# Attention with normed q and k, then a squared-ReLU product: another order of work in the first twelve pairs of heads

## The chip, the cores and the metric

The kernel runs on one core of a Trainium2 chip. The metric is the time of one execution on the device in microseconds (us); of several executions the median is taken. All times below are in us unless marked ns.

## The reference

q, k and v have 8 batches, 12 heads, 448 rows and 64 columns. q and k are normed row by row, attention is a plain softmax, and the heads side by side are the input of a two-layer product.

```python
def rmsnorm(x, g):
    return x / np.sqrt(np.mean(x * x, axis=-1, keepdims=True) + 1e-06) * g
q_n, k_n = rmsnorm(q, g_q), rmsnorm(k, g_k)
scores = np.matmul(q_n, k_n.transpose(0, 1, 3, 2)) / np.sqrt(64)
attn = softmax(scores)                       # exp, divided by its sum
x = heads_side_by_side(attn @ v)             # (8*448, 768)
h = np.maximum(x @ w_in, 0.0)                # w_in (768, 2048)
out = (h * h) @ w_out                        # w_out (2048, 768)
```

q, k and v come as 4-byte floats. w_in and w_out come as 8-byte floats, so the kernel takes each number apart into two 4-byte words and makes a 4-byte float of it on the chip.

## The kernel before, in words

**Tiling.** Two heads are a pair: 48 pairs in all, 6 per batch. Two batches make a span, so there are 4 spans of 12 pairs. Keys are cut into four chunks of 112. `scores(i, c)` (L748) computes for chunk c of pair i the two heads' scores into one of two banks of PSUM and turns them into exponentials with ScalarE. In the first 12 pairs the scale of k sits in that exponential (L759), so k is transposed raw and only q is normed beforehand. `values(i, chunks)` (L805) multiplies exponentials with v into `pav`; `add_up(i, c)` (L766, one VectorE add at L769) sums exponentials over chunks; `total_of(i)` (L813) sums the result over keys with a matmul against ones (L819); `finish(i)` (L822) inverts the sum and scales `pav` into `xT` (L832 to L839); `combine_x(i)` (L842) makes differences of `xT` that the product needs. The `pav` of even pairs lies in a bank of its own, that of odd pairs in bank "n", one of two banks ("m", "n") that the transposes of pairs and, later, the product use as well (`bank`, L456).

**The two products** of a span work with seven products of half-size blocks in place of eight (A11, S2, S1, S3, A12, A22, S4), on a 2 by 2 partition of weights and inputs. `first_product` (L956) has 8 rounds (f) of 7 steps, 56 steps of six matmul records each (L989). `second_product` (L1012) follows. Their weight blocks are streamed from DRAM into five buffers `sw` by `load_blocks` (L637, transfer at L651).

**Weights.** Before they can be streamed they must be made once. `prepare(t)` (L548) is one tick: it takes weight piece t (128 rows, 768 numbers of 8 bytes) through its steps. A tick is cut into four quarters, and `weights(upto)` (L622) runs quarters until that many have been issued. Quarter 1 has the write of a finished pair of pieces to DRAM (L588) and one VectorE step (L593); quarter 2 a ScalarE step (L596) and a VectorE step (L598); quarter 3 a VectorE step (L603) and GpSimd work on the pieces before (L574, L568); quarter 4 a ScalarE step for the next piece (L580), GpSimd work (L568, L574) and the loads of further pieces. The last tick, number 34, ends at quarter 140 (`ALL`). Pieces wait in words buffers: one place in `gC`, two in `gT` and the others in a pool.

**The order of the work** is written out by hand: every engine runs its own instructions in the order in which the program issues them, and waits on semaphores for the others. `attention_alone` (L856) issues the first 12 pairs (NAT = 12) and yields four times per pair. The caller (L1093) runs quarters of weights at each yield, up to `EARLY`. After that `first_product` for span 0 runs the rest of the quarters, spread over its steps (L1105). In all later spans attention is mixed with the second product by another function (L898).

In `attention_alone`, before the change, the first weights are loaded by SP's queue ahead of pair 2, and one tick of weights is issued (`weights(4)`, L1092) ahead of the first scores. Inside pair i come: the loads of pair i+3, scores 0 and 1, `norm(i+2)`, the add of chunk 1, a yield; then the k transpose of pair i+1, the rest of the values and the sum of pair i-1, the q transpose of pair i+1 (L742), `finish(i-1)`, the load of v, a yield; then scores 2 and 3, the first half of the values, a yield; then the add of chunk 2, `combine_x(i-1)`, a yield.

`norm(i)` (L689) squares q and k on ScalarE (L698), sums them on VectorE (L699, L700), takes the power -1/2 on GpSimd (L702) and multiplies q on GpSimd (L704). For pair 1 `normalise_in_turn` (L328) does q first and then k, each with half the work (L332 to L335), and multiplies q on VectorE (L338). From pair 12 on `norm` takes another way (L713: L718 to L726). SP's transfers for pair i+3 (L315, L325) write over what pair i+1 has used, so they wait for its norm.

Of the kernel before, what the change touches and what calls it, by code (L numbers as in the profile page):

```python
# [9 lines left out]
F32 = mybir.dt.float32  # L10
# [376 lines left out]
def attention_then_ffn_bounded(  # L387
# [37 lines left out]
    B, H, S, D = q.shape  # L425
    NT, DM = out.shape
    DFF = w_in.shape[1]
    P = 128
    NJ = 4
# [50 lines left out]
    stage = gC.rearrange("p i f n -> p (i f n)")  # L480
    NW = NPAIR * P
    HW = HC * P
    WORDS, BLOCKS, EXPS, LAST = 6, 2, 4, 31

    EARLY, ALL = 4 * 13, 4 * (2 * NFC + 3)
    assert DM == NW and BLOCKS * 8 * HW + EXPS * NW + 2 * NW <= 3 * HF * S and 2 * NW <= 4 * S and HF % 4 == 0


# [7 lines left out]
        both = words.rearrange("p (n two) -> p n two", two=2)  # L496
        return both[:, :, 0], both[:, :, 1]

    def place_of(n):

        return n % WORDS if n < LAST else 3

    def words_of(n):
        place = place_of(n)
        if place == 0:
            at = BLOCKS * 8 * HW + EXPS * NW
            flat = stage[:, at:at + 2 * NW]
        elif place < 3:
            f = (NFC, HF)[place - 1] - 2
            flat = gT[:, f:f + 2, :].rearrange("p f n -> p (f n)")[:, 0:2 * NW]  # L510
        else:
# [28 lines left out]

    def load_words(t, done):

        while loaded[0] <= t + 3 and all(
                place_of(m) != place_of(loaded[0]) for m in range(max(done, 0), loaded[0])):
            load_w(loaded[0])
            loaded[0] += 1

# [141 lines left out]
    def norm(i):  # L689
        if i >= NAT:  # L690
            squares(i)
            return norm_by_squares(i)
        raw, sq = (places_of(qk, i, n)[:SP] for n in range(2))
        rstd = rstds[i] = small.tile([SP, 2, 2 * NJ], F32, tag="rstd", name="rstd", bufs=4)
        normed[i] = sq[:, 0], raw[:, 1]
        if i == 1:
            return normalise_in_turn(nc, raw, sq, rstd, mhalf)
        nc.scalar.activation(sq, raw, AF.Square)  # L698
        nc.vector.tensor_reduce(rstd, sq.rearrange("p s (n d) -> p s n d", d=D), AX, ALU.add)  # L699
        nc.vector.tensor_scalar(rstd, rstd, 1.0 / D, 1e-6, ALU.mult, ALU.add)  # L700
        flat = rstd.rearrange("p s n -> p (s n)")
        nc.gpsimd.tensor_tensor(flat, flat, mhalf[:SP, 0:4 * NJ], ALU.pow)  # L702

        nc.gpsimd.tensor_tensor(sq[:, 0].rearrange("p (j h d) -> p h j d", j=NJ, h=2),  # L704
                                raw[:, 0].rearrange("p (h j d) -> p h j d", j=NJ, h=2),
                                rstd[:, 0].rearrange("p (h j) -> p h j ()", h=2).to_broadcast([SP, 2, NJ, D]),
                                ALU.mult)
# [55 lines left out]
    def acc_of(i):  # L763
        return sums[i % 2] if i < NAT else sums["acc"]
# [48 lines left out]
    def total_of(i):  # L813


        tots[i] = ps_o.tile([P, S], F32, tag="t", name="tot")
        for n, pr in enumerate((acc_of(i)[:SP], probs[i, NJ - 1])):
            for h in range(2):
                nc.tensor.matmul(tots[i][h * D:(h + 1) * D, :], sums["ones"], pr[:, h, :],  # L819
                                 start=(n == 0), stop=(n == 1))  # L820

    def finish(i):  # L822

        b, hp = divmod(i, NPAIR)
        pav, factors = pavs.pop(i), xT[:, b % 2, hp]
        x = factors
        if i < NAT:


            turned, factors = sums["turned"], sums["factors"]  # L830
            few = small.tile([P, S // 32], F32, tag="few", name="few")
            nc.vector.transpose(turned, tots.pop(i))  # L832
            nc.vector.reciprocal(few, turned.rearrange("p (g r) -> p g r", r=32)[:, :, 0])
            nc.vector.transpose(factors.rearrange("p (g r) -> p g r", r=32),
                                few.rearrange("p g -> p g ()").to_broadcast([P, S // 32, 32]))

            x = x.rearrange("d (p j) -> d j p", j=NJ)
            pav, factors = (t.rearrange("d (j p) -> d j p", j=NJ) for t in (pav, factors))
        nc.vector.tensor_tensor(x, pav, factors, ALU.mult)  # L839
        del vs[i]  # L840
# [15 lines left out]
    def attention_alone():  # L856


        for i in range(NAT):
            more = i + 1 < NAT  # L860
            if i + 3 < NAT:
                load(i + 3)
            scores(i, 0)
            scores(i, 1)
            if i + 2 < NAT:
                norm(i + 2)
            elif not more:
                norm(NAT)
                load(NAT + 2)
            add_up(i, 1)  # L870
            yield
            if i:
                transpose(i + 1, 1, 0) if more else None
                values(i - 1, (2, 3))
                total_of(i - 1)
                transpose(i + 1, 0, 0) if more else None
                finish(i - 1)
            load_v(i + 1)
            yield
            scores(i, 2)  # L880
            scores(i, 3)
            if i == 0:
                transpose(1, 0, 0)
                transpose(1, 1, 1)
            values(i, (0, 1))
            yield
            add_up(i, 2)
            if i:
                combine_x(i - 1)
            if NAT <= i + 3 < NAT + 2:  # L890
                load(i + 3)
            yield
        values(i, (2, 3))
        total_of(i)
        finish(i)
        combine_x(i)

# [58 lines left out]
    def first_product(work, span):  # L956
# [11 lines left out]
        for f in range(HF):  # L968
            n = span * (N1 + N2) + f * 7
            g11, g12 = gT[:, f, 0:S], gT[:, f, S:2 * S]  # L970
            g21, g22 = gT[:, HF + f, 0:S], gT[:, HF + f, S:2 * S]
            add = nc.vector.tensor_tensor
            ps_of = {}
            for i in range(7):

                into, rhs = {A11: ("pa", B11), S2: ("pb", T2), S1: ("pc", T1), S3: ("pd", T3),
                             A12: ("pa", B21), A22: ("pd", T4), S4: ("pc", B22)}[i]
                first = into not in ps_of
                if first and into == "pa":
                    if span == 0 and f:  # L980
                        ps_of[into] = ps_o.tile([P, S], F32, tag="ot"[f % 2], name="pa")
                    else:
                        ps_of[into] = ps_s.tile([P, 2, 512], F32, tag="s", name="pa")[:, 0, 0:S]
                elif first:
                    ps_of[into] = bank(into)
                ps = ps_of[into]
                load_blocks(n + i + 5)
                for c in range(HC):
                    nc.tensor.matmul(ps, stream[n + i][:, c], rhs[:, c], start=first and c == 0,  # L989
                                     stop=c == HC - 1, skip_group_check=not first)  # L990
                if i == A11:
                    p1 = work.tile([P, S], F32, tag="p1", name="p1")
                    nc.scalar.copy(p1, ps)
                elif i == S2:
                    z = work.tile([P, S], F32, tag="z", name="z")
                    add(z, p1, ps, ALU.add)
                elif i == S1:
                    y = work.tile([P, S], F32, tag="y", name="y")
                    add(y, z, ps, ALU.add)
                elif i == A12:  # L1000
                    activate(g11, ps)
                else:
                    g, x = {S3: (g22, y), A22: (g21, z), S4: (g12, z)}[i]
                    add(g, x, ps, ALU.add)  # L1004
                    activate(g, g)
                if span and f and i in (S1, A22):
                    combine(f - 1, (int(i == A22),))
                if span and f == HF - 1 and i == S4:
                    combine(f)
                yield  # L1010
# [65 lines left out]
            squares(nxt + 2)  # L1076

    with tc.tile_pool(name="words", bufs=2) as spare["pool"]:
        for _ in range(2):
            load_w(loaded[0])  # L1080
            loaded[0] += 1
        load(2)
        norm(1)
        with tc.tile_pool(name="first", bufs=2, reuse_waits="tile") as work:

# [3 lines left out]
            sums["turned"], sums["factors"] = (g[:, 0:S] for g in free[2 * NJ + 2:2 * NJ + 4])  # L1089
            sums["ones"] = work.tile([SP, D], F32, tag="ones", name="ones", bufs=1)  # L1090
            nc.vector.memset(sums["ones"], 1.0)
            weights(4)  # L1092
            for u, _ in enumerate(attention_alone()):  # L1093


                weights(min(EARLY, 8 + (EARLY - 8) * (u + 1) // (4 * NAT - 4)))
                if u == 4 * NAT - 6:
                    load_blocks(5)
        with tc.tile_pool(name="first_product", bufs=2, reuse_waits="tile") as work:
            for u, _ in enumerate(first_product(work, 0)):  # L1100
# [120 lines left out]
```

## Time and profile before

| what | value |
| --- | --- |
| median of 5 executions | 1404.55 us (1402.75 to 1405.62) |
| the profiled execution | 1402.9 us |
| its span (first to last instruction) | 1401.1 us |
| granted clock of TensorE, mean | 0.996 |
| busy: PE, DVE, ACT, POOL | 1374.8, 807.2, 420.4, 589.4 us |
| attention alone, to the first step of the product | 0 to 137.87 us |
| first product of span 0 | 137.87 to 264.9 us |
| PE waits before 140 us: for L759, L704, L769, L744 | 5.4, 5.0, 3.0, 1.7 us |

PE is TensorE's matmul side, PEld its weight loads, DVE VectorE, ACT ScalarE, POOL GpSimd, and SPq is SyncE's queue, which issues transfers. "PE pt L742 <- POOL qk L704" means: PE stood still in front of the instruction of line 742 that writes `pt`, and what ended the wait was GpSimd's instruction of line 704. A line of the timeline has start, length, engine, line, operation, tiles written and read, shapes and a count; several instructions of one kind in a row are put together. In a table of stretches each row has the stretch, its length, and for each engine the busy time in it. PEclk is the share of the full clock that TensorE was granted. The profiled execution's 1402.9 us are 1.8 us more than its span.

### The profile page before, as it was taken

How to read it: one execution, taken by the hardware profiler on the slowest of the kernel's cores; microseconds unless marked ns; L12 is line 12 of the kernel's file. 1: busy time of each engine (PE TensorE's matmuls, PEld its weight loads, DVE VectorE, ACT ScalarE, POOL GpSimd, SP SyncE). 2: the span in 40 equal slices, each digit the busy share in tenths (PEclk: the TensorE clock that was granted, in tenths of full speed). 3: DMA queues.
4: the chain of work that ended last, by engine and by line, in shares of the span. 5: the costliest groups of instructions: out<-in, count | busy, mean ns of one | idle time of the engine just before them, and what ended most of it. 6: DMA issues, size and time to landing. Idle time of an engine off the chain costs nothing.

```text
span 1401.1 us, 14407 instructions
## 1 busy us (share of the span) xinstructions
PE 1374.8 (98%) x4422; PEld 636.1 (45%) x4422; DVE 807.2 (58%) x1402; ACT 420.4 (30%) x620; POOL 589.4 (42%) x400
## 2 busy tenths in 40 slices
PE   6998999999999999999999999999999999999998
PEld 2333455444444454544444455444444445554553
DVE  6899677589876234477767523457777633332111
ACT  7884555433322011233232011232323201110000
POOL 7999688544452123544353122545445302221000
PEclk9999999999999999999999999999999999999999
DMA  8767899545755423345576432344564343323443
GB/s 243 219 201 192 300 388 328 158 98 119 142 112 117 101 85 90 102 106 120 116 140 120 96 95 87 101 106 105 124 128 103 94 100 88 90 87 102 107 110 72
DMA packets 430915, 188.78 MB, mean 135 GB/s; under 512 B 277485, under 2 KB 428781, under 8 KB 430829
## 3 DMA queue, kind: packets, MB, share of 16 engines
q1 hardware_dynamic: 421228, 179.05, 49.3%
q10 hardware_dynamic: 9472, 8.72, 2.3%
q8 instruction: 37, 0.61, 0.2%
q14 instruction: 50, 0.40, 0.1%
q0 software_dynamic: 128, 0.00, 0.0%
HBM read 154.54 MB, written 33.16 MB: 134 GB/s over the span
## 4 chain that ended last, share of the span: by engine, by line
PE 92%; POOL 3%; DVE 2%; ACT 1%; issue 1%; DMA 1%; SPq 0%; POOLq 0%; ACTq 0%
PE ps L1036 37%; PE pd L989 10%; PE pa L989 10%; PE pc L989 10%; PE sc L754 10%; PE pav L810 9%; PE pb L989 5%; POOL rstd L702 1%; POOL gC L568 1%; PE tot L819 1%; ACT gT L759 1%; DMA gT<-in_moe_w_in_dram 0%; DVE gT L769 0%; POOL qk L704 0%; PE pt L742 0%
## 5 line engine op out<-in xcount | busy, mean ns | idle before, releaser
L1036 PE MATMUL ps<-gT,sw 128*128 128x448 f32 x768 | 299.2, 542 | 0.8 <-POOL gT L966 0.8
L724 POOL TENSOR_TENSOR half<-half,mhalf 128x28 f32<-128x28 f32 x36 | 173.7, 4826 | 261.6 <-DVE half L723 229.5
L966 POOL TENSOR_TENSOR gT<-gT 128x448 f32<-128x448 f32 x96 | 95.4, 995 | 309.4 <-ACT gT L962 309.4
L1036 PE MATMUL ps<-gC,sw 128*128 128x448 f32 x576 | 225.2, 542 | 0.0
L1036 PEld LDWEIGHTS ps<-gT,sw 128*128 128x128 f32 x768 | 143.9, 190 | 150.9 <-issue 146.9
L761 ACT ACTIVATE pr<-sc 112x896 f32<-112x896 f32 x120 | 104.8, 914 | 294.6 <-PE sc L754 200.6
L754 PE MATMUL sc<-qkT 64*112 64x448 f32 x768 | 170.5, 563 | 7.8 <-ACT gT L759 5.4
L1036 PEld LDWEIGHTS ps<-gC,sw 128*128 128x128 f32 x576 | 108.0, 190 | 112.3 <-issue 111.5
L989 PE MATMUL pa<-xT,sw 128*128 128x448 f32 x384 | 155.1, 540 | 0.0
L962 ACT ACTIVATE gT<-gT 128x448 f32<-128x448 f32 x96 | 55.3, 576 | 307.9 <-DVE gT L1004 307.8
L754 PEld LDWEIGHTS sc<-qkT 64*112 64x112 f32 x768 | 61.4, 173 | 105.4 <-issue 80.2
L989 PEld LDWEIGHTS pa<-xT,sw 128*128 128x128 f32 x384 | 73.1, 191 | 72.4 <-issue 71.8
L810 PE MATMUL pav<-pr,vt 112*64 112x448 f32 x480 | 100.2, 547 | 0.0
L726 POOL TENSOR_TENSOR qk<-qk,half 128x448 f32<-128x448 f32 x72 | 83.7, 1182 | 2.8
L769 DVE TENSOR_TENSOR acc<-acc,pr 112x896 f32<-112x896 f32 x60 | 68.5, 1141 | 19.6 <-ACT pr L761 16.7
L989 PE MATMUL pd<-xT,sw 128*128 128x448 f32 x192 | 77.8, 541 | 0.0
L989 PE MATMUL pb<-xC,sw 128*128 128x448 f32 x192 | 77.5, 540 | 0.1
L1004 DVE TENSOR_TENSOR gT<-z,pd 128x448 f32<-128x448 f32 x32 | 19.8, 620 | 100.1 <-PE pd L989 100.1
L989 PE MATMUL pc<-xT,sw 128*128 128x448 f32 x192 | 77.4, 539 | 0.0
L989 PE MATMUL pc<-xC,sw 128*128 128x448 f32 x192 | 77.4, 539 | 0.0
L989 PE MATMUL pd<-xC,sw 128*128 128x448 f32 x192 | 77.4, 539 | 0.0
L574 POOL TENSOR_TENSOR gC<-gC 128x384 f32<-128x384 f32 x64 | 73.1, 1159 | 2.5
(120 smaller groups left out, 1553.2 us busy)
## 6 DMA issues: line engine op xcount, KB each, us to landing
sw<-w1s SPq DMA_DIRECT2D x224, 192.0 KB, 2.3
sw<-w2s SPq DMA_DIRECT2D x168, 256.0 KB, 3.2
w1s<-gC SPq DMA_DIRECT2D x8, 1344.0 KB, 7.5
w2s<-gC SPq DMA_DIRECT2D x8, 1344.0 KB, 7.5
out_dram<-osb SPq DMA_DIRECT2D x184, 56.0 KB, 1.9
qk<-in_q_dram SPq DMA_DIRECT2D x144, 56.0 KB, 2.9
qk<-in_k_dram SPq DMA_DIRECT2D x144, 56.0 KB, 2.8
vt<-in_v_dram SPq DMA_DIRECT2D x72, 112.0 KB, 2.8
```

Of the source, the lines that this page charges most:

```text
L574: nc.gpsimd.tensor_tensor(*[blocks_of(n)[:, i] for i in (dst, x, y)], op)
L724: nc.gpsimd.tensor_tensor(half, half, mhalf, ALU.pow)
L726: nc.gpsimd.tensor_tensor(qkn[:, s], raw[:, s], half[:, s * NG:(s + 1) * NG].rearrange("p g -> p g ()").to_broadcast([P, NG, 32]), ALU.mult)
L754: nc.tensor.matmul(sc[:, h, 0:S], qkT[rows, at, 1, c * SP:(c + 1) * SP], qkT[rows, at, 0, :], start=True, stop=True)
L761: nc.scalar.activation(pr, sc[:, :, 0:S], AF.Exp)
L769: nc.vector.tensor_tensor(acc, probs[i, 0] if c == 1 else acc, probs[i, c], ALU.add)
L810: nc.tensor.matmul(pavs[i][h * D:(h + 1) * D, :], vs[i][:, h, c, :], probs[i, c][:, h, :], start=(c == 0), stop=(c == NJ - 1))
L962: nc.scalar.activation(g, src, AF.Relu)
L966: nc.gpsimd.tensor_tensor(g, g, g, ALU.mult)
L989: nc.tensor.matmul(ps, stream[n + i][:, c], rhs[:, c], start=first and c == 0, stop=c == HC - 1, skip_group_check=not first)
L1004: add(g, x, ps, ALU.add)
L1036: nc.tensor.matmul(ps, stream[n][:, c % 4], rhs_of[i][:, c], start=c == 0, stop=c == HF - 1)
```

## The change

Six edits, all in the part before the second product of span 0.

1. Pair 2's loads are issued ahead of the first two weight pieces, and no tick of weights stands ahead of the first scores. The first four quarters come after the first pair's only yield.
2. `norm(2)` goes through `normalise_in_turn`, like `norm(1)`.
3. `attention_alone` has another order. Pair 0 has one yield. It issues scores 0 and 1, pair 1's k transpose, scores 2 and 3, pair 1's q transpose, both adds, `norm(2)`, the load of v, half of the values and the loads of pair 3. In later pairs the k transpose, the rest of the values and the sum of pair i-1 and the add of chunk 1 come ahead of `norm(i+2)` and the first yield.
4. `EARLY` goes from 52 to 48 quarters, so one tick moves into the first product. The quarters are spread to the last pair: after yield u, `4 + 44 * u // 41` have been issued.
5. The words buffers go from 6 to 7, and a piece is loaded up to four ticks ahead instead of three. `few` and `p1` get one buffer instead of two.
6. Pair 11 has no add of chunk 2; `total_of(11)` sums the accumulated chunks 0 and 1 and the chunks 2 and 3 by themselves, six matmuls instead of four.

```diff
-    WORDS, BLOCKS, EXPS, LAST = 6, 2, 4, 31
-    EARLY, ALL = 4 * 13, 4 * (2 * NFC + 3)
+    WORDS, BLOCKS, EXPS = 7, 2, 4
+    EARLY, ALL = 4 * 12, 4 * (2 * NFC + 3)
...
-        return n % WORDS if n < LAST else 3
...
-        place = place_of(n)
+        place = n % WORDS
...
-        while loaded[0] <= t + 3 and all(
-                place_of(m) != place_of(loaded[0]) for m in range(max(done, 0), loaded[0])):
+        while loaded[0] <= t + WORDS - 3 and loaded[0] < max(done, 0) + WORDS:
...
-        if i == 1:
+        if i <= 2:
             return normalise_in_turn(nc, raw, sq, rstd, mhalf)
...
-        for n, pr in enumerate((acc_of(i)[:SP], probs[i, NJ - 1])):
+        parts = [acc_of(i)[:SP]] + [probs[i, c] for c in range(2 if i + 1 == NAT else 3, NJ)]
+        for n, pr in enumerate(parts):
...
-                                 start=(n == 0), stop=(n == 1))
+                                 start=(n == 0), stop=(n + 1 == len(parts)))
...
-            few = small.tile([P, S // 32], F32, tag="few", name="few")
+            few = small.tile([P, S // 32], F32, tag="few", name="few", bufs=1)
...
             more = i + 1 < NAT
+            scores(i, 0)
+            scores(i, 1)
+            if i == 0:
+                transpose(1, 1, 1)
+                scores(0, 2)
+                scores(0, 3)
+                transpose(1, 0, 0)
+                add_up(0, 1)
+                add_up(0, 2)
+                norm(2)
+                load_v(1)
+                values(0, (0, 1))
+                load(3)
+                yield
+                continue
+            if more:
+                transpose(i + 1, 1, 0)
             if i + 3 < NAT:
                 load(i + 3)
-            scores(i, 0)
-            scores(i, 1)
+            values(i - 1, (2, 3))
+            total_of(i - 1)
+            add_up(i, 1)
             if i + 2 < NAT:
                 norm(i + 2)
             elif not more:
                 norm(NAT)
                 load(NAT + 2)
-            add_up(i, 1)
             yield
-            if i:
-                transpose(i + 1, 1, 0) if more else None
-                values(i - 1, (2, 3))
-                total_of(i - 1)
-                transpose(i + 1, 0, 0) if more else None
-                finish(i - 1)
+            if more:
+                transpose(i + 1, 0, 0)
+            finish(i - 1)
             load_v(i + 1)
             yield
             scores(i, 2)
             scores(i, 3)
-            if i == 0:
-                transpose(1, 0, 0)
-                transpose(1, 1, 1)
             values(i, (0, 1))
             yield
-            add_up(i, 2)
-            if i:
-                combine_x(i - 1)
+            if more:
+                add_up(i, 2)
+            combine_x(i - 1)
...
-                    p1 = work.tile([P, S], F32, tag="p1", name="p1")
+                    p1 = work.tile([P, S], F32, tag="p1", name="p1", bufs=1)
...
+        load(2)
         for _ in range(2):
             load_w(loaded[0])
             loaded[0] += 1
-        load(2)
         norm(1)
...
-            weights(4)
             for u, _ in enumerate(attention_alone()):
-                weights(min(EARLY, 8 + (EARLY - 8) * (u + 1) // (4 * NAT - 4)))
-                if u == 4 * NAT - 6:
+                weights(min(EARLY, 4 + (EARLY - 4) * u // (4 * NAT - 7)))
+                if u == 4 * NAT - 9:
                     load_blocks(5)
```

More of the change, by code (lines that the diff above doesn't have):

```diff
@@ L497, in pairs_of @@
         return both[:, :, 0], both[:, :, 1]
-    def place_of(n):
-        return n % WORDS if n < LAST else 3
     def words_of(n):
-        place = place_of(n)
+        place = n % WORDS
         if place == 0:
```

## The prediction

> **What bounds the kernel now.** I read the table of engines and the 40 slices first, then the waits of PE (TensorE), then PE in order of time, then the pairs one by one as stretches.
>
> ```profile
> PE 1374.8 (98%) x4422; PEld 636.1 (45%) x4422; DVE 807.2 (58%) x1402; ACT 420.4 (30%) x620; POOL 589.4 (42%) x400
> ...
> PE   6998999999999999999999999999999999999998
> ...
> PEclk9999999999999999999999999999999999999999
> ```
>
> PE is busy for 98% of the span, and from the fifth slice on no digit but the last is under 9. 1401.1 - 1374.8 leaves 26.3 us, 7 of which are the output's tail behind the last matmul (1394.35). What can be won without taking matmuls away lies in the first 140 us, where attention runs alone. Who holds PE there (total, times, longest):
>
> ```profile
> PE sc L754 <- ACT gT L759: 5.4, 1, 5.4
> PE pt L742 <- POOL qk L704: 5.0, 7, 1.4
> PE tot L819 <- DVE gT L769: 3.0, 1, 3.0
> ...
> PE sc L754 <- ACT qkT L744: 1.7, 1, 1.7
> ```
>
> 15.1 us in four waits: ScalarE's exponentials once, GpSimd's normed q seven times, VectorE's running sum once, a copied k once. In order of time the first and the last of these are (start, length, line):
>
> ```profile
> 8.88 1.76 PE L754 MATMUL sc<-qkT 64*112 64x448 f32 x8 [0.77 <-ACT qkT L383]
> 16.03 3.19 PE L754 MATMUL sc<-qkT 64*112 64x448 f32 x8 [5.38 <-ACT gT L759]
> ...
> 23.47 1.76 PE L754 MATMUL sc<-qkT 64*112 64x448 f32 x8 [1.68 <-ACT qkT L744]
> ```
>
> Scores (0,0),(0,1) end at 10.64; the next start at 16.03, because the exponentials that free the score banks begin only at 14.83: ahead of them in ScalarE's order stand the first weights (L580 at 11.32, L596 at 12.11, L580 at 14.02), two of them waiting for transfers. Pair 1 starts at 23.47. From there a pair costs PE 9.26 when nothing waits (23.47 to 32.73); later ones take:
>
> ```profile
> 32.73:42.13 9.40, 9.40 (x50) 3.51 (x48) 8.66 (x13) 7.92 (x14) 9.32 (x7) 1.00 0.24 64
> ...
> 51.40:60.90 9.50, 9.33 (x51) 3.50 (x49) 8.65 (x11) 7.92 (x14) 9.34 (x7) 1.00 0.53 148
> ...
> 70.47:80.29 9.82, 9.55 (x51) 3.52 (x49) 9.22 (x14) 7.93 (x14) 9.66 (x7) 1.00 0.49 142
> ...
> 90.59:101.01 10.42, 9.32 (x50) 3.54 (x48) 9.75 (x14) 7.92 (x14) 10.26 (x7) 1.00 0.46 138
> ```
>
> The columns are start:end, length, then the busy time of PE, weight loads, DVE (VectorE), ACT (ScalarE), POOL (GpSimd). See POOL: 9.32 of 9.40, 9.34 of 9.50, 9.66 of 9.82, 10.26 of 10.42. GpSimd is never idle, so it sets the pair, with VectorE (9.75 of 10.42) close behind.
>
> **Step 1, the start.** Now the four exponentials of scores (0,0),(0,1) follow the squares of pair 1, which end at 10.01; their scales are there at 9.91 (L335, 8.27+1.64). Four took 2.19, so 10.05 to 12.25. ScalarE goes on: k copy of pair 1 0.55 (12.8), four exponentials 2.2 (15.0), scaled q copy 0.63 (15.65; its q is normed at 12.99, L338). Scores (1,0) start at 15.7 instead of 23.47: 7.8 won. The weights come next instead: squares of pair 2 1.15, then a whole tick, L580, L596, L580 at 0.9, so the exponentials of pair 1 run from 19.5. A pair costs ScalarE 4.4+0.55+1.07+0.63+0.92+0.92 = 8.5, those of pair 2 begin at 28.0, and PE waits 1.2 for score banks. VectorE does add (1,2) only at 31.0, after tick 0 (0.55+0.6+0.96), add, norm 3, finish 0 (2.6) and tick 1, so the sum of pair 1 waits 0.8. Scores (3,0) come at 36.2 against 42.13: **5.9 kept** (bounds 4.5 and 7.8). On SP pair 2's three loads pass the first two weights: L315 waits for L338 (7.39), so the weights go out at 9.4 and 9.9 instead of 6.57 and 7.07. They took 4.7 and 6.9 to land, 14.1 and 16.8 by that, and are wanted at 16.8 and 18.6: nothing, up to 1.5 if transfers queue longer. Later pair loads are issued behind PE's transposes, but wait for L704 before and after (47.7 us of SP's waits): nothing.
>
> **Step 2, pairs 3 to 11.** By the end of pair 0 the old order had issued three ticks of weights (12 quarters), the new one issues one. That takes four L568 and two L574 (25.41 to 33.54) away from in front of norm 3 on GpSimd. Pair 2's norm in halves costs GpSimd 2x1.64 instead of 4.14+1.71, VectorE one L338 (0.69) and a second small reduce. Norm 3's L702 now waits for VectorE and starts at 25.2 instead of 33.54: GpSimd is 8.3 ahead where PE is 5.9 ahead. From there it does the work it did before, eight norms and eight ticks (44 quarters in 41 steps). From pair 5 on it follows itself again: norm 5 at 43.4 against 52.62. The last normed q went to PE at 118.18, so 109.0 to 109.8 now. PE, at 9.3 a pair up to pair 6 and 9.5 to 9.9 after that (VectorE's 9.26 to 9.78), is there at 108.1 and waits for 1.3. Adding before norm and copying k before the squares moves 0.5 about between ScalarE and VectorE: nothing. Scores (11,0): 109.4+3.9 = 113.3 against 122.06, **8.8 in all**. Bounds: every pair at 9.26 gives 110.3 (11.8), the old periods from 36.2 give 116.1 (5.9).
>
> **Step 3, the end.** The last sum no longer waits for add (11,2): two matmuls more (four took 1.60, so 0.8), one add less (1.07). PE alone needs 1.69+1.65+1.5+1.69+3.2+2.4 = 12.2 from scores (11,0). What is late next? The old end:
>
> ```profile
> 133.61 1.07 DVE L769 TENSOR_TENSOR gT<-gT 112x896 f32<-112x896 f32 x1
> ...
> 134.83 3.12 PE L819 MATMUL tot<-gT,ones 112*64 112x448 f32 x8 [3.00 <-DVE gT L769]
> ...
> 139.62 0.98 DVE L839 TENSOR_TENSOR xT<-pav,gT 128x448 f32<-128x448 f32 x1
> ...
> 140.70 2.49 PE L989 MATMUL pb<-xC,sw 128*128 128x448 f32 x6
> ```
>
> Pair 11's pav sits in bank "n", and so does the first pb of the product: pb cannot start before L839 has read pav (it ended at 140.60; pb 140.70). Behind pb, PE's whole product is queued. VectorE's queue up to that L839 loses one add but gains an L603 (0.96 to 1.65) and an L598 (0.55 to 1.1), as weights now run into the last pair. Before, it worked from 122.09 to 136.41 without a stop, 14.3; now 14.8 to 16.0, and the finish 2.6: L839 ends 17.4 to 18.7 after scores (11,0). PE could start pb at 12.2+2.25 = 14.45. I take 17.6: **a gap of 3.1 moves from the sum to pb**. The clock decides what it costs (third column from the end):
>
> ```profile
> 22.00:23.00 1.00, 0.00 (x0) 0.00 (x0) 0.97 (x3) 1.00 (x3) 1.00 (x1) 1.00 1.09 387
> ...
> 135.00:136.00 1.00, 1.00 (x4) 0.33 (x3) 0.97 (x3) 0.00 (x0) 0.93 (x1) 0.51 0.53 185
> ...
> 138.00:139.00 1.00, 1.00 (x3) 0.58 (x4) 0.93 (x3) 0.00 (x0) 1.00 (x2) 0.79 0.49 82
> ```
>
> A gap of 1.68 left 1.00; one of 3.00 was followed by 0.51, 0.50, 0.50, 0.79, which is 1.7 lost. Mine is nearest to the second: 1.7. The product's fourth step then starts 17.6+4.5+1.7 = 23.8 after scores (11,0), before 23.2 (145.29-122.06): the end gives **back 0.6**. Bounds: 4.3 won without a wait at pb, 1.7 lost at 18.7. [...]
>
> SP bounds the same point: behind load 14 (L670), which waits for GpSimd's L726 of norm 12, stands the sixth block (L651 at 142.34). VectorE's L723 comes some 9 after scores (11,0) instead of 8.2, so the block is some 8 earlier, as PE is: no more than 1 either way.
>
> **Step 4, the first product** takes one tick more (92 quarters for 88 in 50 steps). PE is 100% busy there, GpSimd 81%, VectorE 73%: nothing. The seventh words buffer brings each weight a tick sooner; no engine waits for words after 15 us: 0, at most 1. p1 and few with one buffer: p1 is written every 15.8 us and read 2.6 later: 0. Words 29 and 30 now lie where f=6 writes; GpSimd was done with both by 241.83, f=6 writes at 242.61 and 244.72, and the pace there is the same: 0, with little margin.
>
> **Sum.** 8.8 - 0.6 = 8.2. The profiled execution took 1402.9 (1.8 around its span), so 1394.7; it lies 1.65 below the median 1404.55, so on the median **1396.4**.
>
> **Rivals.** (a) PE's pace throughout: 11.8 won by pair 11, 0 to 4.3 at the end: 1388.5 to 1392.5. For it: little work is new. Against it: POOL's 10.26 a pair. 0.12. (b) The lead is eaten: weights late at the start (1.5), old periods in pairs 3 to 11, an end that gives back 1.7: 2 to 5.5 won, 1399 to 1402.5. For it: VectorE at 9.75 a pair. 0.16, of which 0.13 over 2.8. (c) The waits only change names, within 2.8: 0.05. (d) Slower: the product's blocks starve. A step of 2.255 us moves 0.197 MB of blocks and 0.44 tick of 1.44 MB, 0.83 MB; now 0.46, 0.86 MB.
>
> ```profile
> 160.00:180.00 20.00, 20.00 (x55) 10.15 (x54) 15.14 (x22) 11.22 (x18) 16.27 (x16) 1.00 1.01 371
> 180.00:200.00 20.00, 20.00 (x55) 10.15 (x54) 13.63 (x18) 13.55 (x21) 16.56 (x17) 1.00 1.04 392
> ```
>
> Last two columns: the transfer engines' share, 1.01 and 1.04, and GB/s, 371 and 392. 0.86 MB at 381 just fits a step. Under 340 each of 40 steps costs 0.3 more, 12 us, more than the gain: 1408 and above. Against it: blocks landed in 5.8, with a lead of 9. 0.07.
>
> **How the numbers follow.** Forecast (6 to 11 won, 1393.5 to 1398.5) 0.60, rivals as given. Faster by over 0.2% (2.8 us, about what a measurement can tell): 0.60+0.12+0.13 = 0.85; same 0.03+0.05 = 0.08; slower 0.07. The range 1390.5 to 1401.5 leaves out a third of (a), a quarter of (b), (c) and (d): 0.20.
>
> **What would show it.** Right: no PE gap at 11 to 16; scores (1,0) near 15.7, (11,0) near 113; "PE pt <- POOL qk" well under 5.0; no wait of the last sum, but pb behind L839. Wrong: scores (3,0) after 38, PE pausing in L989 for sw, or a product that starts within 5 us of 137.87.

## The result and the profile after

The changed kernel takes 1401.74 us (median of 27 runs), the kernel before 1404.65 beside it (47 runs): a ratio of 0.998, 95% interval 0.9974 to 0.9985, so 2.9 us were won where 8.2 were forecast. The profiled execution took 1399.1 with a span of 1397.3, 3.8 under that of before. It is a fast one: the 27 counted executions go from 1399.27 to 1405.85. Every kernel here has one trace, so a difference of one to three us between two traces is a sign and no more. In the changed kernel the scores are L749, the exponentials L754, the k copy L739, the pairs' sum L815, the finish L828 to L835, the combine L848 to L850, the product L997, the weights' write L583 and their load L532.

The waits of PE up to 150 us (total, times, longest) are these:

```profile
PE tot L815 <- DVE gT L764: 2.7, 3, 1.3
PE pt L737 <- POOL qk L699: 2.0, 2, 1.2
...
PE pav L805 <- DMA vt<-in_v_dram: 1.7, 2, 1.2
PE pb L997 <- issue: 1.5, 1, 1.5
```

The wait for the exponentials (5.4) is down to 0.6 and that for the normed q from 5.0 to 2.0. New are waits for transfers of v and the one in front of pb. PE in order of time (start, length):

```profile
15.16 1.76 PE L749 MATMUL sc<-qkT 64*112 64x448 f32 x8
...
124.14 4.00 PE L805 MATMUL pav<-gT,vt 112*64 112x448 f32 x16 [1.23 <-DMA vt<-in_v_dram]
128.04 2.48 PE L815 MATMUL tot<-gT,ones 112*64 112x448 f32 x12
...
134.43 2.49 PE L997 MATMUL pb<-xC,sw 128*128 128x448 f32 x6 [1.46 <-issue]
```

Scores (1,0) start at 15.16 for 23.47. The last sum (128.04) waits for nothing; pb does. Further marks divide the way:

| mark | before | after | earlier by |
|---|---|---|---|
| scores (3,0) | 42.13 | 35.98 | 6.15 |
| scores (11,0) | 122.06 | 116.31 | 5.75 |
| product's fourth step (pd) | 145.29 | 139.02 | 6.27 |
| second product's first scores | 264.91 | 260.75 | 4.16 |
| end of the span | 1401.1 | 1397.3 | 3.8 |

The start won its 6. The eight pairs from 3 to 10 won nothing (80.33 for 79.93), the end won another 0.5, and the product gave 2.1 back (121.73 from pd to the second product's first scores, for 119.62). Behind those scores all 14 traces of this document take 1136.2 to 1136.7 us, so the kernels differ ahead of them.

**Where the pairs stand.** Stretches from scores (i,0) to scores (i+1,0), i from 4 (columns as in the prediction's tables):

```profile
45.37:54.63 9.26, 9.26 (x51) 3.56 (x49) 9.09 (x12) 7.90 (x14) 9.18 (x6) 1.00 0.30 91
...
73.33:83.85 10.52, 9.45 (x50) 3.60 (x48) 6.10 (x9) 6.84 (x12) 10.14 (x8) 1.00 1.09 284
...
94.09:106.13 12.04, 9.54 (x50) 3.50 (x48) 11.77 (x18) 8.00 (x14) 11.69 (x7) 1.00 1.02 277
```

Pairs 4 and 5 run at PE's own 9.26; from pair 7 on they take 10.2 to 12.0. VectorE's 6.10 of 10.52 in pair 7 tells that it was short of input there, not of time. In pair 9 it is the other way round: VectorE is busy for 11.77 of 12.04 us and GpSimd for 11.69, so these rows alone leave open whether the two engines or the transfers are to blame. ScalarE, which squares q and k first, did wait for transfers of k (after, up to 145 us):

```profile
ACT qk L693 <- DMA qk<-in_k_dram: 6.6, 3, 3.3
...
ACT qk L706 <- DMA qk<-in_k_dram: 3.6, 1, 3.6
```

The waits of SP's queue up to 145 us, before and then after (L588 and L583 are the write, L315 the loads of q):

```profile
SPq L315 <- POOL qk L704: 47.7, 8, 8.8
SPq L588 <- POOL gC L574: 12.2, 5, 6.8
```

```profile
SPq L583 <- POOL gC L569: 35.1, 4, 15.2
SPq L315 <- POOL qk L699: 24.9, 5, 8.2
```

SP's queue around the first slow pair, after:

```profile
61.83 0.45 SPq L532 DMA_DIRECT2D gT<-in_moe_w_in_dram  x1
71.73 0.38 SPq L583 DMA_DIRECT2D w1s<-gC  x1
72.21 0.51 SPq L315 DMA_DIRECT2D qk<-in_q_dram  x1
```

SP stood in front of the write from 62.3 to 71.73; the next pair's loads are directly behind it. The pace of the quarters explains the order. At one quarter for each yield, the quarter that holds a write is issued behind a pair's first yield, behind that pair's loads. The change issues 44 quarters over 41 yields. From yield 14 it is one quarter ahead, and then the write is issued after the last yield of the pair before, in front of the loads.

**The product.** Its stretch from 140 to 160 us, before, then after:

```profile
140.00:160.00 20.00, 19.95 (x54) 9.76 (x53) 12.58 (x17) 9.77 (x16) 11.65 (x11) 1.00 0.81 252
```

```profile
140.00:160.00 20.00, 19.13 (x50) 9.06 (x49) 14.33 (x18) 11.80 (x19) 16.47 (x15) 1.00 1.06 391
```

The transfer engines' share goes from 0.81 to 1.06, and PE loses 0.8 of the 20 us: it waits for blocks ("PE pa L997 <- DMA sw<-w1s: 0.5", "pd: 0.4"). Over 130 to 250 us the median landing of a block went from 4.7 to 6.2 us. Before has a share of 1.01 to 1.04 too, but only from 160 us on, and its PE pauses nowhere behind pd.

### The profile page after: what moved, and what is told of

It reads as the page before. It is cut to its first block, busy times and chain, and to the rows that moved or that the text cites. A ratio compares the mean times of both kernels' runs of the same rounds, so it can differ in the third digit from the quotient of the medians.

```text
span 1397.3 us, 14398 instructions
## 1 busy us (share of the span) xinstructions
PE 1375.2 (98%) x4426; PEld 634.9 (45%) x4426; DVE 808.7 (58%) x1404; ACT 420.4 (30%) x621; POOL 589.7 (42%) x400
## 4 chain that ended last, share of the span: by engine, by line
PE 92%; DMA 3%; POOL 3%; DVE 1%; issue 0%; SPq 0%; ACT 0%; POOLq 0%
PE ps L1044 37%; PE pd L997 10%; PE pa L997 10%; PE pc L997 10%; PE sc L749 10%; PE pav L805 9%; PE pb L997 5%; DMA sw<-w1s 1%; POOL rstd L697 1%; POOL qk L699 1%; PE tot L815 1%; DMA qk<-in_q_dram 1%; DMA vt<-in_v_dram 1%; DMA gT<-in_moe_w_in_dram 1%; POOL gC L563 1%
## 5 line engine op out<-in xcount | busy, mean ns | idle before, releaser
L719 POOL TENSOR_TENSOR half<-half,mhalf 128x28 f32<-128x28 f32 x36 | 173.6, 4822 | 262.4 <-DVE half L718 229.9
L749 PE MATMUL sc<-qkT 64*112 64x448 f32 x768 | 169.6, 559 | 1.5 <-ACT qkT L383 0.8
L997 PE MATMUL pa<-xT,sw 128*128 128x448 f32 x384 | 155.0, 540 | 0.5 <-DMA sw<-w1s 0.5
L997 PEld LDWEIGHTS pa<-xT,sw 128*128 128x128 f32 x384 | 72.8, 190 | 72.5 <-issue 71.2
L749 PEld LDWEIGHTS sc<-qkT 64*112 64x112 f32 x768 | 60.8, 172 | 98.7 <-issue 80.8
L721 POOL TENSOR_TENSOR qk<-qk,half 128x448 f32<-128x448 f32 x72 | 84.7, 1196 | 2.8
L997 PE MATMUL pb<-xC,sw 128*128 128x448 f32 x192 | 77.5, 540 | 1.5 <-issue 1.5
L1012 DVE TENSOR_TENSOR gT<-z,pd 128x448 f32<-128x448 f32 x32 | 19.9, 620 | 101.5 <-PE pd L997 101.5
L997 PE MATMUL pd<-xT,sw 128*128 128x448 f32 x192 | 78.1, 543 | 0.0
L997 PE MATMUL pd<-xC,sw 128*128 128x448 f32 x192 | 77.5, 539 | 0.4 <-DMA sw<-w1s 0.4
L997 PE MATMUL pc<-xT,sw 128*128 128x448 f32 x192 | 77.5, 540 | 0.0
L997 PE MATMUL pc<-xC,sw 128*128 128x448 f32 x192 | 77.4, 539 | 0.0
L569 POOL TENSOR_TENSOR gC<-gC 128x384 f32<-128x384 f32 x64 | 70.4, 1118 | 2.5
```

What stands on the lines that cost most here:

```text
L569: nc.gpsimd.tensor_tensor(*[blocks_of(n)[:, i] for i in (dst, x, y)], op)
L719: nc.gpsimd.tensor_tensor(half, half, mhalf, ALU.pow)
L721: nc.gpsimd.tensor_tensor(qkn[:, s], raw[:, s], half[:, s * NG:(s + 1) * NG].rearrange("p g -> p g ()").to_broadcast([P, NG, 32]), ALU.mult)
L749: nc.tensor.matmul(sc[:, h, 0:S], qkT[rows, at, 1, c * SP:(c + 1) * SP], qkT[rows, at, 0, :], start=True, stop=True)
```

## The experiments

Times are ratios to the kernel before on the same chip, with the 95% interval. Theory A is the order on SP just read, theory B that VectorE and GpSimd slow each other when the pairs come faster, theory C that transfers fill their engines in the product and starve the blocks. "The product" is the stretch from the fourth step to the second product's first scores. Some traces are far from the median of their kernel: 3.2 us slower for the old order of the pairs, 2.1 for thirteen ticks, 1.7 for one tick alone and for the quiet end, 2.8 faster for both.

**Even pace.** From the changed kernel, one quarter for each yield:

```diff
-                weights(min(EARLY, 4 + (EARLY - 4) * u // (4 * NAT - 7)))
+                weights(min(EARLY, 4 + u))
```

> The changed kernel with one line altered: one quarter of weights per yield (4 + u, up to 48) instead of 4 + 44*u//41, so that the quarter that issues the write of a finished pair to DRAM again follows a pair's loads on SP's queue instead of standing ahead of them. Theory A (SP's order: the write, which waits for GpSimd, holds the loads of q, k and v behind it): SP's wait at the write falls from 35.1 us in the first 145 us to under 15, ScalarE no longer waits for k's transfers (6.6 + 3.6 in the changed kernel), scores (11,0) come at 112 to 113.5 instead of 116.31, and the time is about 3 us below the changed kernel, some 1398.7, a ratio to the kernel before of 0.995 to 0.9965. Theory B (VectorE and GpSimd slow each other and eat the lead, the transfers only come late because of that): scores (11,0) stay at 115 to 117, the ratio stays at 0.998.

0.9962 (0.9948 to 0.9976). Scores (11,0) start at 110.79, every pair from 4 to 9 takes 9.26, and SP's waits up to 145 us are:

```profile
SPq L315 <- POOL qk L699: 38.6, 7, 8.2
SPq L583 <- POOL gC L569: 9.1, 3, 7.0
```

35.1 became 9.1. The write itself goes out when it did (71.41 for 71.73), but the loads of q are now ahead of it, 3.6 us earlier than in the changed kernel:

```profile
68.64 0.31 SPq L315 DMA_DIRECT2D qk<-in_q_dram  x1
...
71.41 0.39 SPq L583 DMA_DIRECT2D w1s<-gC  x1
```

Pair 9, which took 12.04:

```profile
92.03:101.29 9.26, 9.26 (x50) 3.59 (x48) 9.09 (x13) 7.90 (x14) 9.03 (x7) 1.00 1.09 278
```

Theory A holds, with scores (11,0) even ahead of its 112 to 113.5, and B falls: the same work of VectorE and GpSimd fits into 9.26 us, and PE waits for nothing. Seven of the kernels below keep this pace through most of the pairs, and their traces have scores (11,0) at 110.5 to 112.7, all well ahead of 116.31. The edit moves all work of the weights by one to three yields, though, and not the write alone; a kernel that moves only the write was not run. But the fourth step starts at 137.71, only 1.3 earlier than after. The end, from PE in order of time (the last sum waits 1.65 ahead of these lines):

```profile
131.58 4.04 PE L997 MATMUL pb<-xC,sw 128*128 128x448 f32 x6 [3.48 <-issue]
135.45 2.42 PE L997 MATMUL pc<-xC,sw 128*128 128x448 f32 x6
```

PE stands 3.48 in front of pb, released at the end of VectorE's L835 (131.48), and pb to pc takes 3.87 instead of 2.33: the clock granted over 120 to 140 us is 0.91. The product takes 123.2. So the 5.5 us won in the pairs were given back at the end (4.2) and in the product (1.5); the profiled span is 1397.5, as after. The trace of the change lies 2.6 under its median, however: by the medians the even pace is 5.4 us under the kernel before and the change 2.9. Their intervals just touch.

**Old order of the pairs.** The even-pace kernel with the order of pairs 1 to 11 and the last sum as before:

```diff
-        parts = [acc_of(i)[:SP]] + [probs[i, c] for c in range(2 if i + 1 == NAT else 3, NJ)]
+        parts = [acc_of(i)[:SP], probs[i, NJ - 1]]
...
-            values(i - 1, (2, 3))
-            total_of(i - 1)
-            add_up(i, 1)
             if i + 2 < NAT:
                 norm(i + 2)
             elif not more:
                 norm(NAT)
                 load(NAT + 2)
+            add_up(i, 1)
```

> Even pace as in the run before, and pairs 1 to 11 and the last sum in the order of the kernel before; what stays of the change is the start (pair 0, loads, norm 2 in halves), 12 ticks and 7 words buffers. Theory A: the start carries nearly the whole gain; scores (11,0) within 1 us of the even-paced run, the wait of the last sum for add (11,2) is back with 2 to 3 us, and the ratio is 0.995 to 0.9975. Theory B: the old order of the pairs gives the old periods, scores (11,0) at 115 or later, ratio 0.998 or more.

0.9967 (0.9954 to 0.998). Scores (11,0) come at 116.14, 5.4 behind the even-pace kernel, so in these two traces the new order of the pairs is worth that with an even pace. Theory A was wrong here: it gave the start nearly the whole gain and expected scores (11,0) within 1 us; 116.14 is what B expected of this kernel (115 or later). The write is not what holds them, since SP waits only 8.3 us for it. The last sum waits again, 4.9 us where 2 to 3 were expected:

```profile
PE tot L815 <- DVE gT L764: 7.4, 4, 4.9
```

The fourth step is at 141.80, 4.1 later than with the new order, yet the medians are 0.7 us apart, within their intervals. The trace is the slowest of its six executions (1402.97, median 1399.75), so the 5.4 and the 4.1 may be too large.

**A later load.** The even-pace kernel with the last load of the pairs at the product's step 12:

```diff
                 norm(NAT)
-                load(NAT + 2)
...
+                if u == 12:
+                    load(NAT + 2)
```

> The even-paced kernel with the loads of pair 14 moved from the last pair into step 12 of the first product, so that the sixth weight block no longer waits on SP behind them. Theory A for the product (SP's order again, the blocks start late): the product's steps no longer pause for sw, fourth step to second product in 119.8 us instead of 121.7, ratio 1 us (0.0007) below the even-paced run. Theory C (the transfers' engines are full in the product, one tick more than before): the pauses stay, the time is that of the even-paced run.

0.9983 (0.9971 to 0.9995), some 3 us slower than the even-pace kernel, which neither theory expected. In its trace 1.9 us are already lost at scores (11,0), ahead of the edit, so a part of it is a difference between executions. The product takes 123.8 with 2.6 us of waits of pd for blocks, the longest 1.3, so the load's place on SP's queue is not what starves the product.

**One tick alone.** The kernel before, with nothing but its thirteenth tick moved into the product:

```diff
-    EARLY, ALL = 4 * 13, 4 * (2 * NFC + 3)
+    EARLY, ALL = 4 * 12, 4 * (2 * NFC + 3)
...
-                weights(min(EARLY, 8 + (EARLY - 8) * (u + 1) // (4 * NAT - 4)))
+                weights(min(EARLY, 9 + u))
```

> The kernel before with one edit alone: the thirteenth tick goes from pair 10 into the first product (48 quarters before it instead of 52), all else as before. Theory C (the tick fills the product's transfers): PE pauses for sw in the product by 1 to 2 us in all, and the ratio is 1.000 to 1.001. Theory A: no pause over 0.3 us in the product; the last two pairs lose GpSimd and VectorE work, the product starts 0.5 to 2 us earlier, ratio 0.9985 to 1.000.

1.0 (0.9991 to 1.0009). The product takes 122.9 us for 119.6, and PE, which waited for nothing in before's product, now has:

```profile
PE pd L989 <- DMA sw<-w1s: 1.0, 1, 1.0
PE pa L989 <- DMA sw<-w1s: 0.4, 1, 0.4
```

So 3.3 are lost there with nothing moved but the tick; beside these 1.4 and 0.4 for VectorE's z, the pauses lie inside steps, where no wait is named. This trace is the slowest of its 12 (1406.44, median 1404.78). It is 3.5 behind before at scores (9,0) already (104.52 for 101.01), where the two kernels are still the same. From there to the fourth step it takes 40.95 for 44.28: the tick taken out of the pairs wins 3.3 and loses 3.3 in the product, which agrees with the ratio of 1.0.

**The norm of the next pair, later.** The even-pace kernel with pair 12's norm and the load behind it late in the first product, to see what makes VectorE late in front of pb (theory V):

```diff
-            elif not more:
-                norm(NAT)
-                load(NAT + 2)
...
+                if u == N1 - 16:
+                    norm(NAT)
+                if u == N1 - 14:
+                    load(NAT + 2)
```

> The even-pace kernel with the norm and the squares load of the first pair of the product moved from the end of the pairs into the first product (steps N1-16 and N1-14). Theory V (the second step of the product waits for VectorE's finish of pair 11, which stands late because that norm is queued ahead of it): VectorE is free earlier by the norm's some 3 us, PE's 3.5 us gap at pb falls under 1 us, the half clock behind it goes (another 1.5 us), and the fourth step comes 4 to 5 us earlier than 137.7, at 132.7 to 134. Rival (the finish is late for the running sum's own length, not for the norm): gap 2.5 to 3.5, fourth step at 136.5 to 138. For the total: if the product is limited by the transfers (theory C), it starts earlier but its pauses stay, 123 to 124 from the fourth step to the second product's first scores, total 394.5 to 396.5 past 1000, so 1394.5 to 1396.5; if the rival holds, 1398.5 to 1400.

0.9999 (0.999 to 1.0008). Theory V falls, and its rival's numbers miss too: the gap grows to 4.9, and the fourth step comes at 139.45. VectorE in the even-pace kernel, then here:

```profile
127.05 0.62 DVE L849 TENSOR_TENSOR xC<-xT,xC 128x448 f32<-128x448 f32 x1
```

```profile
126.61 1.32 DVE L849 TENSOR_TENSOR xC<-xT,xC 128x448 f32<-128x448 f32 x1
```

The combine took 1.32 for 0.62, and the weights' L598 1.66 for 0.96, now that GpSimd does the weights' adds beside them (L563 from 122.90 to 125.22 and from 126.17 on) instead of the norm's power -1/2. The same stretch of VectorE's work, from L588 to pair 11's L835, began 1.45 earlier and ended 0.3 later. The product takes 126.5 us with the norm in it.

**Thirteen ticks.** The even-pace kernel with two ticks behind pair 0:

```diff
-    EARLY, ALL = 4 * 12, 4 * (2 * NFC + 3)
+    EARLY, ALL = 4 * 13, 4 * (2 * NFC + 3)
...
-                weights(min(EARLY, 4 + u))
+                weights(min(EARLY, 8 + u))
```

> The even-pace kernel with thirteen ticks of weights ahead of the product, as in the kernel before, two of them behind pair 0. Theory C (the tick moved into the product fills the transfers' engines and starves the blocks): from the fourth step to the second product's first scores 119.5 to 120.5 instead of 123.2; at the start the second tick holds ScalarE's exponentials of pair 1 for 1 to 3 us; total 1396 to 1398.5. Rival (the pauses come from something else that the new pairs bring, such as the order on SP): product 122.5 to 124, total 1399 to 1402.

0.9986 (0.9976 to 0.9996). The second tick costs more than either theory said:

```profile
PE pt L737 <- ACT qkT L739: 6.2, 1, 6.2
```

ScalarE stood 3.6 us for a piece of weights with pair 1's exponentials behind it. And the product takes 122.2, 1.0 less than with twelve ticks, where theory C expected 119.5 to 120.5. Blocks still cause 1.5 us of waits, so the count of ticks alone doesn't set the pauses.

**Both.** The two edits above together:

> Both of the above, the later norm and thirteen ticks. If theories V and C both hold and their gains add: fourth step at 133 to 136, product 119.5 to 120.5, total 1392 to 1395. If the later norm only moves the wait into the product (its norm and its load then compete there): no better than the better of the two alone.

1.0039 (1.0023 to 1.0054), slower than either alone. The gap in front of pb is 4.9, the wait of the 13-tick start 4.5, and the product takes 125.6: the losses came together, and neither hoped-for gain.

**Half of the words.** The even-pace kernel without 14 of the weights' loads (the expectation says which):

```diff
+            if n >= 20 and n % 2 == 0:
+                return
             f = n % NFC // 2 + n % 2 * HF
```

> The even-pace kernel that leaves out the load of every second piece of weights from the twentieth on (the words already in place are used instead, so those weights are not the reference's): 14 loads less in the first product, all other instructions the same. Theory C (transfers' engines full): the landing times of the blocks fall back to a median of 4.5 or less, the pauses of PE go, and from the fourth step to the second product's first scores takes 118.5 to 120 instead of 123.2; total 1395 to 1397. Rival (the pauses come from the work of the weights on ScalarE, VectorE or GpSimd, or from the writes and their order on SP): product 122 to 124, total 1398.5 to 1400.

0.9947 (0.9934 to 0.996). Blocks' transfers over 130 to 250 us (count, KB, median us to landing), in the even-pace kernel and here:

```profile
sw<-w1s SPq DMA_DIRECT2D x51, 192.0 KB, 6.5
```

```profile
sw<-w1s SPq DMA_DIRECT2D x51, 192.0 KB, 4.3
```

PE waits for no block any more, and the product takes 121.35. That is between the two expectations: 1.8 under the even-pace kernel and 1.7 over before's 119.6, and 1.4 of the latter is one wait for VectorE's L1016 (0.6 in the even-pace kernel, L1012 there). The edit takes transfers off SP's queue as well as bytes off the engines, but the landing of a block is counted from its issue, and that fell from 6.5 to 4.3. So the waits for blocks come with the other transfers in flight, as C says.

**A quiet end.** The even-pace kernel with no weights in the last four steps of the pairs (theory Q: VectorE's queue as a whole sets pb):

```diff
-                weights(min(EARLY, 4 + u))
+                weights(min(40, 4 + u))
```

> The even-pace kernel with the quarters of the weights stopped at 40 (ten ticks), so that the last four steps of the pairs carry none; the quarters left out there are caught up at the first product's first step. Theory Q (VectorE's queue as a whole sets the second step of the product: finish of pair 10, three weights instructions, combine of pair 10, finish and combine of pair 11, 9.5 us without a pause in the even-pace kernel): without the three weights instructions, 2.1 us, the finish of pair 11 ends at 129 to 129.7 instead of 131.48, the gap at the second step falls from 3.5 to 1.0 to 1.7, no half clock follows, fourth step at 133.5 to 135 instead of 137.71. Rival (what VectorE is spared there is eaten by longer instructions or by what it waits for, as when the norm was moved): fourth step at 136.5 to 138. The product starts with a tick more to do: by theory C (transfers' engines full) 124 to 126.5 from the fourth step to the second product's first scores instead of 123.2. Total within 2 us of the even-pace kernel, that is 1398 to 1402.

0.9958 (0.9944 to 0.9971). pb starts at 126.00, 5.6 earlier, behind a gap of 0.31. The three instructions left out are 2.1 of that. Of the rest of VectorE's queue, pair 10's L850 took 0.62 beside GpSimd's power (L719, 118.01 to 122.82), for 1.36 beside its multiplying (L721, 127.30 to 129.75) in the even-pace kernel. Then the quarters are caught up in the product's first two steps, and PE pays behind them:

```profile
PE pd L997 <- DVE z L1004: 4.3, 1, 4.3
```

VectorE there:

```profile
129.79 1.35 DVE L588 TENSOR_SCALAR gC<-gC 128x768 f32<-128x768 f32 x1
...
133.89 0.56 DVE L593 TENSOR_SCALAR gC<-gC 128x768 uint32<-128x768 uint32 x1
134.37 0.61 DVE L1004 TENSOR_TENSOR z<-p,pb 128x448 f32<-128x448 f32 x1
```

From 129.79 on, z stands behind five weights instructions (1.35, 1.23, 0.96, 0.55 and 0.56, 4.7 us). So VectorE's queue set pb (Q), made longer by GpSimd's work beside it, and the catch-up is the same cause in a new place. The fourth step is at 135.04, and the product takes 125.9, within what theory C expected (124 to 126.5).

**The other bank.** The even-pace kernel with the banks of the product's first steps exchanged:

```diff
+            turn[0] += 1
             for u, _ in enumerate(first_product(work, 0)):
```

> The even-pace kernel with the two banks of the first product's first steps exchanged, so that its second step takes the bank that pair 11's pav doesn't hold. If the held bank alone makes the wait (the prediction's third step): the second step starts right behind the first, some 3 us earlier, no half clock, fourth step at 133.5 to 135. If VectorE's queue sets it (theory Q): the second step's first matmuls start earlier, but its last ones still wait for the combine of pair 11 on VectorE, which ends at 133.5; fourth step at 136 to 137.5, total within 1.5 us of the even-pace kernel.

0.9949 (0.9936 to 0.9963). pb starts at 128.40, right behind pa, so the held bank did set its start. Its last matmuls then wait for VectorE:

```profile
PE pb L997 <- DVE xC L848: 2.6, 1, 2.6
```

The clock stays at 1.00, the fourth step is at 135.91. The bank is worth 1.8 of the end, the queue the rest. The product takes 124.5, 1.3 more than with the even pace, with 2.7 us of waits for blocks.

**Quiet end and other bank.**

> Both of the above. If bank and queue each hold a part: fourth step at 131.5 to 133.5. The total, by theory C, 0 to 3 us under the even-pace kernel, since the product begins earlier but with a tick more to do.

0.9951 (0.9937 to 0.9964). pb at 124.84, but z still stands behind the catch-up (4.5): fourth step 134.35, product 122.9.

**Smooth.** The last kernel, with the product's share spread from 40 quarters on:

```diff
-                weights(min(ALL, EARLY + (ALL - EARLY) * (u - 1) // (N1 - 6)))
+                weights(min(ALL, 40 + (ALL - 40) * max(0, u - 2) // (N1 - 7)))
```

> The last kernel (quarters stopped at 40, banks exchanged) with the first product's share spread evenly over its steps from 40 on, none of them at its first two steps, where the last kernel caught up eight quarters at once. Theory Q (VectorE's queue): the fourth step no longer waits for z behind six weights instructions (4.5 us there, of which the half clock before it is a part): second step at 125, fourth step at 129.5 to 131.5 instead of 134.35. Theory C (the transfers' engines are full, so what comes earlier is given back as pauses): from the fourth step to the second product's first scores 124.5 to 127 instead of 122.9, total 1395 to 1398, within 1.5 us of the last kernel. Rival to C (the product has room): 122.5 to 123.5 there, total 1392 to 1394.

**0.9904 (0.9888 to 0.9921)**, 13.5 us under the kernel before, better than both kernels. The end of the pairs and the product's start have no pause left:

```profile
123.51 2.52 PE L997 MATMUL pa<-xT,sw 128*128 128x448 f32 x6
125.87 2.71 PE L997 MATMUL pb<-xC,sw 128*128 128x448 f32 x6
...
130.76 2.52 PE L997 MATMUL pd<-xT,sw 128*128 128x448 f32 x6
```

The product takes 122.5 with two more ticks in it, where C, as a price for each tick, gave 124.5 to 127. In that form C falls: from 140 to 200 us the transfer engines' share is 1.04 to 1.06, and PE has no pause. Blocks still cause waits (1.2 and 0.6 us), only later, from 200 us on.

## Why the prediction was wrong

- **Step 1 (5.9 kept): right.** Scores (1,0) at 15.16 for 15.7, (3,0) at 35.98 for 36.2, 6.15 won. The wait foretold for the sum of pair 1 (0.8) is there with 0.91. The one foretold for pair 2 (1.2, for score banks) is not: a wait of 1.10 came instead in front of pair 2's q transpose, for the copy of k (L739). That its size agrees is luck.
- **Step 2 (8.8 in all): failed**, at the sentence in step 1 that begins "Later pair loads are issued behind PE's transposes, but wait for L704 before and after" and puts them at "nothing". The "44 quarters in 41 steps" were counted for GpSimd and not followed onto SP. There they put the write ahead of the loads: 5.75 in all came instead of 8.8. With an even pace 11.3 came, near the bound of 11.8 that the step gave for PE's pace throughout (9.35 to 11.53 in the eight traces with that pace). So the periods of 9.5 to 9.9, put down to VectorE, were no limit in the new order. Nor does GpSimd set the pair because it is "never idle": it was busy for 10.26 of a 10.42 us pair before and does a pair's work in 9.0 to 9.2 here. Why the old order of the pairs takes longer even at an even pace stays open.
- **Step 3 (a gap of 3.1 moves to pb, 0.6 back): the mechanism was right, its size depended on step 2.** The last sum waits no more and pb starts at 134.43, right behind L835 (133.37+0.96). The gap is 1.46, and the clock stays at 1.00; PE itself had lost time in the pairs and 1.23 to v of pair 11. Where the pairs keep their lead, the even-pace kernel shows the gap of 3.48 and a clock of 0.91 over 20 us. The prediction named the held bank as what holds pb; that was worth 1.8 us, and the rest is VectorE's queue, as the other-bank kernel shows.
- **Step 4 ("nothing"): failed.** "PE is 100% busy there, GpSimd 81%, VectorE 73%" left out the transfers' engines, at 1.01 to 1.04 already. The step lost 2.1 between the two traces, one tick alone 3.3, and with half of the words no wait for a block is left. Rival (d) had the mechanism, with too high a price (12) and too small a chance.
- **The sum** became 6.3 at the fourth step, less 2.1 in the product, less 0.4 behind it, 3.8 in the traces. By the medians it is 2.9, since the trace of the change lies 2.6 under its median and that of before 1.7. The time fell among rival (b)'s, by other causes than it named: the pairs were slow for SP's order and not for VectorE, no engine waited more than 0.6 for late weights at the start, and the end gave nothing back.

What stays open: the order of transfers that leaves before's product without a pause. Neither thirteen ticks nor fewer bring its 119.6 back in the new kernels (121.7 to 126.5, and 121.4 with half of the words). The fifth edit, which loads a piece up to four ticks ahead into seven buffers, is in all of them and was never taken back alone, so it may have a part in this. Nor was the smooth pace tried without the bank exchanged, so how much of its gain needs the bank isn't known.

## What to carry to other kernels

When a pace changes, follow every instruction of each quarter onto every in-order queue: here the writes of finished weights, moved ahead of the loads, cost some 5 us by pair 11, and the busy shares of the engines did not name them. A lead won early is worth only what the next shared queue lets through: here it took an even pace, an end without background work on VectorE, another bank and no catch-up behind it to make 13.5 us out of 2.9. Transfer engines at a share of 1.0 belong in the sum even where every engine has room, but the share alone is no price: 1.06 cost waits in the changed kernel and none in the smooth one.

## What the runs showed of the hardware

- One VectorE instruction, the combine of 128x448, took 0.62 us while GpSimd ran the norm's power on 128x28 (some 5 us), and mostly 1.23 to 1.44 while it ran adds on 128x384. Several combines took 0.61 beside an add that was then the long one (2.4 us, where others take 1.0 to 1.4). VectorE in the smooth kernel:

```profile
121.49 0.62 DVE L849 TENSOR_TENSOR xC<-xT,xC 128x448 f32<-128x448 f32 x1
...
127.54 1.30 DVE L849 TENSOR_TENSOR xC<-xT,xC 128x448 f32<-128x448 f32 x1
```

  GpSimd was in the power (L719) from 118.35 to 123.15 and in the adds (L569) from 127.10 on; the power's 4.80 us held no combine up. Why combines are longer beside the adds, no run here shows.
- A gap of PE of 1.46 us left the clock at 1.00 (changed kernel, 120 to 140 us), and an inner wait of 2.60 in the other-bank kernel did so too. Gaps of 3.46 to 4.95 around the start of the product brought 0.83 to 0.96 over the 20 us from 120 to 140, the 3.00 of before 0.91 there, and one of 1.96 in the late-norm kernel (in front of pb at 232.59) 0.91 over 220 to 240 us. So these traces give no one length of a gap from which the clock falls.
